# Half-block stores in the middle of a fused attention and MLP kernel, and two evacuations on other engines

## The chip, the cores and the metric

The kernel runs on one core of one Trainium2 chip. The metric is the device time of one execution in microseconds; the median of three runs before the change is 215.45 us (215.32 to 215.66).

## The reference

A lightning attention (linear attention with a decay per head, computed in blocks, with a running state) feeds an MLP with an ELU-like activation. Cut to what matters:

```python
# q, k, v: (4, 8, 768, 64); lam: one decay per head
for b in range(nb):                        # blocks along the sequence
    intra = einsum('bhic,bhjc->bhij', qb, kb) * Dmask       # causal, decayed
    intra = einsum('bhij,bhjd->bhid', intra, vb)
    inter = einsum('bhid,bhde->bhie', qb * lam_pow, kv_state)
    out[:, :, sl] = intra + inter
    kv_state = lam_block * kv_state + einsum('bhsd,bhse->bhde', kb * rev_pow, vb)
x = out as (3072 tokens, 512)
h = x @ w_in                               # 512 -> 2048
g = where(h > 0, h, exp(min(h, 0)) - 1)
y = g @ w_out                              # 2048 -> 512, float32, the output
```

## The kernel before, in words

**Tiling.** The 3072 tokens are 24 blocks of 128 (4 batches, 6 blocks of the sequence each, numbered g = 0 to 23). Everything stays on chip between attention and MLP. For a block the attention needs q and k transposed (T), the scores (S, line 302), the weighted values and the state's share (P, lines 338 and 344), and the state's update (U, line 406). The MLP's first matmul `mm1` (line 478) works on pairs of blocks, with an exponential and a ReLU on ScalarE (lines 484, 485) and a combination on VectorE (line 457); its second, `mm2` (line 499), gathers one block's 512 output columns in one PSUM bank in four steps.

**Order.** The order is written out by hand: a list of steps (`prog`) is run from front to back, and every engine executes its instructions in the order in which they were written. `1:g:j` is a step of `mm1`, `2:g:j` one of `mm2`, `S18:19` the scores of two blocks, `B:P18:...` their values and states. `W18` (`pool_work`) issues, for blocks from 8 on, the two transposes of block 18 (its q, then its k) as DMAs on SyncE (line 268); `L20` loads q, k and v of blocks 20 and 21 through GpSimd's queue (line 109). The part of the list around the change reads

```
... 2:12:3 1:14:3 W18 2:13:0 1:14:4 B:P16:P17:U16:U17 2:13:1 1:14:5 W19 2:13:2 1:14:6 L20 2:13:3
1:14:7 2:14:0 1:16:0 S18:19 2:14:1 1:16:1 2:14:2 1:16:2 2:14:3 1:16:3 W20 ...
```

**Stores.** When a block's fourth step of `mm2` is done, `out_of` copies its PSUM bank into an SBUF tile of 128 x 512 (`osb`, four buffers; line 525 on ScalarE) and appends a store to the list `stores`. Nothing is issued there. `mm1` calls `emit_stores(1)` at its beginning, which writes the DMA issues to SyncE (line 450) until one entry is left. A store thus stands in SyncE's order behind the evacuation of the next block, but waits only for its own evacuation. SyncE's order there, with T for two transposes, is: store 11, T18, T19, store 12, store 13, T20, T21, store 14, store 15, T22, T23, store 16 and on.

**The end.** The last block, 23, is computed in two parts: columns 0 to 383 by `mm2` (`CUT`), evacuated on VectorE (line 523), and columns 384 to 511 by `mm2_rest` (line 511), evacuated on ScalarE (line 525). For this block `out_of` issues its store at once.

**Completion.** The framework gives SyncE's DMAs eight landing semaphores in turn (in the trace: 108, 109, 113, 114, 115, 116, 117, 118). A later reader of the data, and a later writer of the tile, waits on the semaphore of the DMA in question. At the end of the program SyncE waits for all semaphores in a fixed order (line 658), among them these eight in the order given, before all engines meet and the program ends.

Of the kernel before, what the change touches and what calls it, by code (L numbers as in the profile page):

```python
# [7 lines left out]
FP32 = mybir.dt.float32  # L8
# [7 lines left out]
def kernel(  # L16
# [11 lines left out]
    nc = tc.nc  # L28

    B, H, S, D = q.shape  # L30
# [7 lines left out]
    FB = 4  # L38
    NJ = NFT // FB
    GPE = 8  # L40
    LAST = NG - 1
    CUT = 384
    GSIZE = {**{g: 1 for g in range(4)}, **{g: 2 for g in range(4, NG, 2)}}
    GFIRST = {g0 + i: g0 for g0, n in GSIZE.items() for i in range(n)}
    WI = [2] * 8
# [22 lines left out]
    TAGS = {w: t.replace(",", " ") for w, t in (x.split("=") for x in BANKS.split())}  # L68
# [7 lines left out]
    ps = ctx.enter_context(tc.tile_pool(name="ps", bufs=1, space=bass.MemoryType.PSUM))  # L76
# [36 lines left out]
    for w in RAW.split():  # L113
        x = {"q": q, "k": k}[w[0]]
        g0 = int(w[1:])
        raw[w] = asb.tile([128, H, 64], FP32, name=f"raw_{w}", tag=f"raw_{w}")
        (nc.sync if w[0] == "q" else nc.scalar).dma_start(
            out=raw[w][:], in_=x[g0, :, 0:L].rearrange("h p d -> p h d")
# [80 lines left out]
    def zero_st1(b):  # L199
# [21 lines left out]
        out=ident16[:], in0=row[:], scalar1=pos[:, 0:1], scalar2=None, op0=ALU.is_equal  # L221
    )
    nc.vector.tensor_scalar(
        out=causT[:], in0=row[:], scalar1=pos[:, 0:1], scalar2=None, op0=ALU.is_ge
# [24 lines left out]
    def bank(what, i, shape, dtype, name):  # L249
        tag = TAGS[what].split()[i]  # L250
        return ps.tile(
            shape, dtype, tag=f"ps{tag}", name=name, bufs=2 if tag == "H" else 1
        )
# [55 lines left out]
    def until(done, g):  # L309
        while g not in done:  # L310
            late.pop(0)()
# [15 lines left out]
    def att_P(g):  # L327
# [21 lines left out]
        def evacuate():  # L349
            g0 = GFIRST[g]  # L350
            n = GSIZE[g0]
            if g0 not in xg:
# [92 lines left out]
    gts, psM, stores, pending = {}, {}, [], []  # L445

    def emit_stores(keep=0):
        while len(stores) > keep:
            dst, o = stores.pop(0)
            nc.sync.dma_start(out=dst, in_=o)  # L450

    def flush():
        while pending:
            g0, j, e, r = pending.pop(0)
            n = GSIZE[g0]
            g = msb.tile([128, FB // n, n, 128], FP16, tag="g", bufs=40, name=f"g{g0}_{j}")
            nc.vector.scalar_tensor_tensor(  # L457
                out=g[:].rearrange("p f c t -> p (f c t)"), in0=e[:], scalar=-1.0, in1=r[:],
                op0=ALU.add, op1=ALU.min,
            )  # L460
            for f in range(FB // n):
                for c in range(n):
                    gts[(g0 + c, j * (FB // n) + f)] = g[:, f, c, :]
        if late:
            late.pop(0)()

    def mm1(g0, j):
        flush()
        emit_stores(1)
        n = GSIZE[g0]  # L470
        assert {f"P{g0 + i}" for i in range(n)} <= seen
        for i in range(n):
            until(X_done, g0 + i)
        pH = ps.tile([128, FB * 128], FP32, tag="psH", bufs=2, name=f"psH{g0}_{j}")
        for f in range(FB // n):
            i, w = wi_of[j * (FB // n) + f]
            for kk in range(NHP):
                nc.tensor.matmul(  # L478
                    pH[:, f * n * 128 : (f + 1) * n * 128],
                    lhsT=wi16[i][:, kk, w * 128 : (w + 1) * 128],  # L480
                    rhs=xg[g0][:, kk, :], start=(kk == 0), stop=(kk == NHP - 1),
                )
        e = msb.tile([128, FB * 128], FP32, tag="e", bufs=3, name=f"e{g0}_{j}")
        nc.scalar.activation(e[:], pH[:], AF.Exp)  # L484
        nc.scalar.activation(pH[:], pH[:], AF.Relu)  # L485
        pending.append((g0, j, e, pH))
# [3 lines left out]
    def mm2(g, j):  # L490
        flush()
        cols = slice(0, CUT if g == LAST else DM)
        if mm2_done[g] == 0:
            psM[g] = bank(f"M{g}", 0, [128, DM], FP32, f"psM{g}")
        first, mm2_done[g] = mm2_done[g] == 0, mm2_done[g] + 1
        end = mm2_done[g] == NJ
        for f in range(FB):
            i, w = wo_of[j * FB + f]
            nc.tensor.matmul(  # L499
                psM[g][:, cols], lhsT=gts[(g, j * FB + f)], rhs=wo16[i][:, w, cols],  # L500
                start=first and f == 0, stop=end and f == FB - 1, skip_group_check=True,
            )
        if end:
            out_of(g, psM[g][:, cols], cols, nc.vector if g == LAST else nc.scalar)

    def mm2_rest():
        cols = slice(CUT, DM)
        rest = ps.tile([128, DM - CUT], FP32, tag="psA", name="psMrest", bufs=1)
        for f in range(NFT):
            i, w = wo_of[f]  # L510
            nc.tensor.matmul(
                rest[:], lhsT=gts[(LAST, f)], rhs=wo16[i][:, w, cols],
                start=f == 0, stop=f == NFT - 1,
            )
        out_of(LAST, rest[:], cols, nc.scalar)

    def out_of(g, src, cols, eng):
        cb, b = divmod(g, B)
        t0 = b * S + cb * L
        w = cols.stop - cols.start  # L520
        o = msb.tile([128, w], FP32, tag=f"osb{w}", bufs=4, name=f"osb{g}_{cols.start}")
        if eng is nc.vector:
            eng.tensor_copy(o[:], src)
        else:
            eng.copy(o[:], src)  # L525
        stores.append((out[t0 : t0 + 128, cols], o[:]))
        if g == LAST:
            emit_stores()

# [26 lines left out]
    def run(t):  # L556
        w, *a = t[0], *t[1:].replace(":", " ").split()
        if w == "B":
            for o in a:
                ready(o)  # L560
            burst(*a)
            return
        a = [int(x) for x in a]
        if w in "PUzZ":
            ready(t)
        if w == "S":
            for g in a:
                att_S(g)
            for g in a:
                late.extend(att_E(g))  # L570
            late.pop(0)()
            late.pop(0)()
        elif w == "P":
            burst(t)
        elif w == "U":
            late.extend(att_U(*a))
            while late:
                late.pop(0)()
        else:
            {"T": att_T_pe, "1": mm1, "2": mm2, "Z": zero_st, "z": zero_st1,  # L580
             "q": lambda g, e: cast_raw(g, "q", e), "k": lambda g, e: cast_raw(g, "k", e),
             "c": lambda i: (emit_qs, emit_mask, emit_ks)[i](), "W": pool_work, "L": load_pair,
             "M": next_M, "w": zero_matmuls}[w](*a)

    for t in FIRST.split():
# [4 lines left out]
    done = set(prog) | {o for t in prog if t[0] == "B" for o in t.split(":")}  # L590
    m1 = [(g, j) for g, n in GSIZE.items() for j in range(NJ * n)]
    place = {u: i for i, u in enumerate(m1)}
    need = {
        (g, j): place[(GFIRST[g], ((j + 1) * FB - 1) // (FB // GSIZE[GFIRST[g]]))]
        for g in range(NG) for j in range(NJ)
# [31 lines left out]
    for t in prog:  # L627
        run(t)
    mm2_rest()
    while late:  # L630
        late.pop(0)()
# [31 lines left out]
```

## Time and profile before

| what | us |
|---|---|
| median of 3 runs | 215.45 |
| profiled execution, first to last instruction (span) | 213.2 |
| TensorE matmuls busy | 202.7 |
| VectorE busy | 130.1 |
| ScalarE busy | 129.0 |
| last matmul's end | 210.1 |
| last store issued | 210.41 |
| last store landed | 212.01 |
| last instruction's end | 213.2 |

The times in profile lines count from the first instruction of the span. Engines are named PE (TensorE matmuls), PEld (its weight loads), DVE (VectorE), ACT (ScalarE), POOL (GpSimd) and SP (SyncE); a q behind the name stands for the engine's sequencer, which issues DMAs and waits. `out<-in` are the names of tiles. In a timeline a row begins with its start and its length. A row with `x2` merges two neighbouring instructions of one kind, and its length then includes the time between them. In a list of waits the numbers are the total, the times and the longest. "DMA to landing" counts from the issue to the arrival of the whole transfer.

### The profile page before, as it was taken

How to read it: one execution, taken by the hardware profiler on the slowest of the kernel's cores; microseconds unless marked ns; L12 is line 12 of the kernel's file. 1: busy time of each engine (PE TensorE's matmuls, PEld its weight loads, DVE VectorE, ACT ScalarE, POOL GpSimd, SP SyncE). 2: the span in 40 equal slices, each digit the busy share in tenths (PEclk: the TensorE clock that was granted, in tenths of full speed). 3: DMA queues.
4: the chain of work that ended last, by engine and by line, in shares of the span. 5: the costliest groups of instructions: out<-in, count | busy, mean ns of one | idle time of the engine just before them, and what ended most of it. 6: DMA issues, size and time to landing. Idle time of an engine off the chain costs nothing.

```text
span 213.2 us, 5156 instructions
## 1 busy us (share of the span) xinstructions
PE 202.7 (95%) x2066; PEld 138.1 (65%) x2066; DVE 130.1 (61%) x224; ACT 129.0 (61%) x245; POOL 96.2 (45%) x115
## 2 busy tenths in 40 slices
PE   7667999999999999999999999999999999999994
PEld 2355676767686776766766766766766666666652
DVE  3936453777846888677667667667667547533321
ACT  4545654884867756676476476476476576477640
POOL 7996991999972908667166259300000000000000
PEclk9999999999999999999999999999999999999999
DMA  8999999999996999999939919999124110110112
GB/s 90 141 175 193 192 148 173 147 165 147 153 165 145 111 197 107 144 122 116 129 106 125 167 59 103 144 180 161 52 65 83 52 49 0 54 51 16 36 49 98
DMA packets 101976, 24.59 MB, mean 115 GB/s; under 512 B 92608, under 2 KB 99008, under 8 KB 101952
## 3 DMA queue, kind: packets, MB, share of 16 engines
q0 software_dynamic: 79760, 13.50, 83.1%
q1 hardware_dynamic: 22192, 10.76, 24.6%
q8 instruction: 16, 0.26, 0.5%
q14 instruction: 8, 0.07, 0.1%
HBM read 27.27 MB, written 6.29 MB: 157 GB/s over the span
## 4 chain that ended last, share of the span: by engine, by line
PE 82%; POOL 8%; DMA 7%; issue 1%; ACT 1%; DVE 0%; POOLq 0%; ACTq 0%
PE psM L499 36%; PE psH L478 35%; DMA wi<-in_moe_w_in_dram 4%; DMA wo<-in_moe_w_out_dram 3%; PE psO L338 3%; PE psS L302 3%; PE psO L344 2%; POOL kd L174 1%; POOL wi L148 1%; POOL kn L109 1%; POOL vn L109 1%; PE psU L406 1%; PE psT L283 1%; POOL qn L109 1%; POOL wo L155 1%
## 5 line engine op out<-in xcount | busy, mean ns | idle before, releaser
L478 PE MATMUL psH<-xt,wi 128*128 128x256 f16 (+1 forms) x896 | 99.3, 258 | 2.0 <-DMA wi<-in_moe_w_in_dram 1.1
L457 DVE SCALAR_TENSOR_TENSOR g<-e,psH 128x512 f16<-128x512 f32 x96 | 65.8, 686 | 56.7 <-ACT psH L485 56.0
L484 ACT ACTIVATE e<-psH 128x512 f32<-128x512 f32 x96 | 57.3, 597 | 65.0 <-PE psH L478 62.8
L499 PE MATMUL psM<-wo,g 128*128 128x512 f16 (+1 forms) x384 | 95.6, 377 | 0.7 <-DMA wo<-in_moe_w_out_dram 0.7
L478 PEld LDWEIGHTS <-wi 128*128 128x128 f16 x896 | 76.9, 98 | 27.4 <-DMA wi<-in_moe_w_in_dram 1.8
L485 ACT ACTIVATE psH<-psH 128x512 f32<-128x512 f32 x96 | 57.0, 593 | 0.0
L499 PEld LDWEIGHTS <-g 128*128 128x128 f16 x384 | 35.9, 98 | 29.3 <-issue 1.3
L318 DVE TENSOR_TENSOR pp<-psS,mask 128x512 f16<-128x512 f32 x48 | 30.8, 684 | 4.4 <-PE psS L302 4.4
L174 POOL TENSOR_TENSOR kd<-kn,ks 128x512 f16<-128x512 f16 x20 | 20.7, 1040 | 21.3 <-DMA kn<-in_k_dram 20.4
L378 POOL TENSOR_TENSOR stt<-st,upp 64x256 f32<-64x256 f16 x32 | 19.5, 608 | 14.7 <-DVE st L418 8.9
L109 POOL DMA_DIRECT2D vn<-in_v_dram x14 | 15.5, 1108 | 1.7 <-DMA wi<-in_moe_w_in_dram 1.7
L109 POOL DMA_DIRECT2D kn<-in_k_dram x14 | 15.5, 1105 | 0.8 <-POOLq L647 0.8
L525 ACT COPY osb<-psM 128x512 f32<-128x512 f32 x23 | 13.5, 590 | 3.2 <-PE psM L499 3.2
L109 POOL DMA_DIRECT2D qn<-in_q_dram x13 | 14.8, 1138 | 0.0
L418 DVE TENSOR_TENSOR st<-stt,psU 64x256 f16<-64x256 f32 x32 | 13.3, 416 | 1.2 <-PE psU L406 0.5
L361 DVE TENSOR_TENSOR xt<-psO,qs 128x512 f16<-128x512 f32 x16 | 11.0, 688 | 3.5 <-PE psO L344 3.5
L338 PE MATMUL psO<-pp,vn 128*64 128x128 f16 x192 | 12.0, 222 | 1.2 <-DMA vn<-in_v_dram 1.0
L338 PEld LDWEIGHTS <-vn 128*64 128x64 f16 x192 | 9.7, 110 | 4.6 <-issue 2.9
L344 PE MATMUL psO<-qT,st 128*64 128x128 f16 x160 | 10.0, 219 | 0.0
L344 PEld LDWEIGHTS <-st 128*64 128x64 f16 x160 | 8.9, 110 | 0.0
L302 PE MATMUL psS<-qT,kT 64*128 64x128 f16 x192 | 7.9, 218 | 0.3 <-ACT kT L291 0.3
L359 ACT CAST xt<-psO 128x512 f16<-128x512 f32 x8 | 4.4, 588 | 6.4 <-PE psO L338 4.3
(44 smaller groups left out, 72.3 us busy)
## 6 DMA issues: line engine op xcount, KB each, us to landing
out_dram<-osb SPq DMA_DIRECT2D x23, 256.0 KB, 2.2
kn<-in_k_dram POOLq DMA_DIRECT2D x10, 256.0 KB, 7.8
qn<-in_q_dram POOLq DMA_DIRECT2D x10, 256.0 KB, 6.8
vn<-in_v_dram POOLq DMA_DIRECT2D x10, 256.0 KB, 7.6
wi<-in_moe_w_in_dram POOLq DMA_DIRECT2D x8, 256.0 KB, 6.9
wo<-in_moe_w_out_dram POOLq DMA_DIRECT2D x8, 256.0 KB, 7.7
kn<-in_k_dram POOLq DMA_DIRECT2D x4, 128.0 KB, 4.2
vn<-in_v_dram POOLq DMA_DIRECT2D x4, 128.0 KB, 5.5
```

The source lines that it names most:

```text
L109: nc.gpsimd.dma_start(out=t[:].rearrange("p b h d -> p (b h) d"), in_=src)
L174: nc.gpsimd.tensor_tensor(out=kd[:], in0=of(kg, g), in1=ks[:].unsqueeze(2).broadcast_to([128, H, 64]), op=ALU.mult,)
L302: nc.tensor.matmul(psS[g][hh][:, hp, :], lhsT=kt[r, hp, :], rhs=qt[r, hp, :], start=True, stop=True,)
L318: nc.vector.tensor_tensor(out=P[:], in0=pts[hh][:], in1=mask[:, hh::2, :], op=ALU.mult)
L338: nc.tensor.matmul(po[r, hp, :], lhsT=vt[:, 2 * hp + hh, :], rhs=Pt[(g, hh)][:, hp, :], start=True, stop=(cb == 0), skip_group_check=True,)
L344: nc.tensor.matmul(po[r, hp, :], lhsT=st[b][cb % 2][:, hp, r], rhs=qt[:, hp, :], start=False, stop=True, skip_group_check=True,)
L378: nc.gpsimd.tensor_tensor(out=tmp[r], in0=old[r, :, r], in1=upp[r].unsqueeze(2).broadcast_to([64, NHP, 64]), op=ALU.mult,)
L457: nc.vector.scalar_tensor_tensor(out=g[:].rearrange("p f c t -> p (f c t)"), in0=e[:], scalar=-1.0, in1=r[:], op0=ALU.add, op1=ALU.min,)
L478: nc.tensor.matmul(pH[:, f * n * 128 : (f + 1) * n * 128], lhsT=wi16[i][:, kk, w * 128 : (w + 1) * 128], rhs=xg[g0][:, kk, :], start=(kk = ...
L484: nc.scalar.activation(e[:], pH[:], AF.Exp)
L485: nc.scalar.activation(pH[:], pH[:], AF.Relu)
L499: nc.tensor.matmul(psM[g][:, cols], lhsT=gts[(g, j * FB + f)], rhs=wo16[i][:, w, cols], start=first and f == 0, stop=end and f == FB - 1, ...
```

## The change

Blocks 12, 14, 15, 16 and 17 append two entries to `stores` in place of one, of 256 columns (128 KB) each; the evacuations are unchanged. The two parts of the last block swap engines: columns 0 to 383 are now copied by ScalarE, columns 384 to 511 by VectorE. A lookup of the PSUM tag for `mm1`'s tile is added; no entry of the table `BANKS` begins with H, so the tile stays where it was.

```diff
     CUT = 384
+    SPLIT = (12, 14, 15, 16, 17)
@@ mm1
-        pH = ps.tile([128, FB * 128], FP32, tag="psH", bufs=2, name=f"psH{g0}_{j}")
+        tag = TAGS.get(f"H{g0}_{j}", "H")
+        pH = ps.tile(
+            [128, FB * 128], FP32, tag=f"ps{tag}", name=f"psH{g0}_{j}",
+            bufs=2 if tag == "H" else 1,
+        )
@@ mm2
-            out_of(g, psM[g][:, cols], cols, nc.vector if g == LAST else nc.scalar)
+            out_of(g, psM[g][:, cols], cols, nc.scalar)
@@ mm2_rest
-        out_of(LAST, rest[:], cols, nc.scalar)
+        out_of(LAST, rest[:], cols, nc.vector)
@@ out_of
-        stores.append((out[t0 : t0 + 128, cols], o[:]))
+        parts = 2 if g in SPLIT else 1
+        for i in range(parts):
+            c = slice(i * w // parts, (i + 1) * w // parts)
+            d = slice(cols.start + c.start, cols.start + c.stop)
+            stores.append((out[t0 : t0 + 128, d], o[:, c]))
         if g == LAST:
             emit_stores()
```

## The prediction

> **What bounds the kernel now.** I read the page first, then the waits of TensorE's neighbours, then SyncE's queue, where the change acts, and last the end of the span.
>
> ```profile
> span 213.2 us, 5156 instructions
> PE 202.7 (95%) x2066; PEld 138.1 (65%) x2066; DVE 130.1 (61%) x224; ACT 129.0 (61%) x245; POOL 96.2 (45%) x115
> PE psM L499 36%; PE psH L478 35%; DMA wi<-in_moe_w_in_dram 4%; DMA wo<-in_moe_w_out_dram 3%; PE psO L338 3%; PE psS L302 3%; PE psO L344 2%; POOL kd L174 1%; POOL wi L148 1%; POOL kn L109 1%; POOL vn L109 1%; PE psU L406 1%; PE psT L283 1%; POOL qn L109 1%; POOL wo L155 1%
> ```
>
> TensorE is busy for 95% and carries the chain. In windows from 90 to 184 us it is busy without a gap, so whatever stops it there comes out at the end in full. ACT and VectorE have slack: in 120 to 204 us they wait 30.5 and 30.2 us for it.
>
> The changed stores are issued by SyncE, which works in program order and spends most of its time blocked (SyncE's waits):
>
> ```profile
> SPq L450 <- ACT osb L525: 131.1, 19, 40.9
> SPq L658 <- DMA out_dram<-osb: 1.1, 2, 0.8
> ```
>
> A store at the head of that queue waits for its evacuation, and everything behind it waits too. Behind some of them stand transposes that TensorE needs. SyncE's timeline (start, length, instruction):
>
> ```profile
> 126.03 0.33 SPq L450 DMA_DIRECT2D out_dram<-osb  x1
> 126.47 1.22 SPq L268 DMA_TRANSPOSE qT<-qn  x1
> 127.78 1.22 SPq L268 DMA_TRANSPOSE kT<-kn  x1
> 129.09 1.22 SPq L268 DMA_TRANSPOSE qT<-qn  x1
> 130.36 1.33 SPq L268 DMA_TRANSPOSE kT<-kn  x1
> 133.64 8.65 SPq L450 DMA_DIRECT2D out_dram<-osb  x2
> 142.39 1.25 SPq L268 DMA_TRANSPOSE qT<-qn  x1
> ```
>
> The store at 126.03 is block 11's; then T18 and T19 (two transposes each); the pair merged from 133.64 is the stores of blocks 12 and 13; T20 begins at 142.39. TensorE needs T18 and T19 here (its timeline), the second half of the 16 matmuls being block 19's, from 143.95:
>
> ```profile
> 143.64 0.62 PE L302 MATMUL psS<-qT,kT 64*128 64x128 f16 x16
> ```
>
> **The end of the span.** The last evacuation ends at 210.38, the 64 KB store issues at 210.41 and lands 1.60 later, at 212.01. SyncE's waits at L658 then go through the landing semaphores in a fixed order. Six start between 212.02 and 212.33, 0.061 apart: the first is the last store's own, the five behind it are for stores and engines long done.
>
> ```profile
> 209.23 0.56 DVE L523 COPY osb<-psM 128x384 f32<-128x384 f32 x1 [4.19 <-PE psM L499]
> 209.81 0.93 SPq L450 DMA_DIRECT2D out_dram<-osb  x2
> 210.12 0.27 ACT L525 COPY osb<-psMrest 128x128 f32<-128x128 f32 x1 [2.91 <-PE psMrest L511]
> ```
>
> **The change part by part.** *The ring.* SyncE issues 59 transfers (25 stores, 32 transposes, 2 loads) over eight landing semaphores in turn; the 59th takes the third. Five halves more make 64, and the 64th takes the eighth. The five waits then pass while the store is under way: 5 x 0.061 = **-0.30 us**.
>
> *The engines.* VectorE has no 128x128 copy out of PSUM in this trace. From its 128x384 copy (0.558) and its 64x256 cast (0.422) the slope is 1.06 ns an element, so 0.422 - 0.136 = 0.286 estimated, against ACT's 0.265: **+0.02** on the path. Bounds: its cast from SBUF (0.228) and its first 128x128 compare (0.377), so -0.04 to +0.11. The 384-column copy on ACT, interpolated between 0.265 and 0.590, is 0.48 against 0.56; its store moves up by 0.08, which is not on the path, but could free the last store's landing, so 0 to -0.08; I take 0. Both engines start 0.02 after TensorE's semaphore.
>
> *Five more issues.* 0.33 us each plus a wait of 0.05, 1.9 us of SyncE in all. SyncE's 68.1 us of waiting for evacuations from 120 us on hides them. ACT's evacuations of blocks 16 and 18 to 21 must wait for two landings instead of one (0.028 against 0.017): hidden in its 30.5 us of waiting. Without that cover all this is under 2.0 us.
>
> *The order on SyncE.* This is the term that decides. `emit_stores(1)` in `mm1` counts entries and leaves one behind. Today block 12's only entry stays behind until block 13 has been evacuated, and the W18 and W19 steps, which issue T18 and T19, are written in between. With two entries the list after block 12's evacuation is 11, 12a, 12b, and the next `mm1`, directly ahead of W18, issues 11 and 12a. So 12a, which must wait for its evacuation, moves **ahead of four transposes**; 14a does the same to T20 and T21, 16a to T22 and T23. 15 and 17 move past nothing.
>
> T18 now starts when 12a is out: 133.64 + 0.43 (the distance from block 11's store to T18) = 134.07 instead of 126.47. With the pitch of 1.30 the fourth is issued at 137.97. What does a transpose take to land? The first group is T19, at 129.09 and 130.36; the second T22 and T23, at 158 to 163:
>
> ```profile
> DMA to landing us min/median/max: 7.5/7.7/7.9
> ...
> DMA to landing us min/median/max: 2.4/2.4/2.5
> ```
>
> T19 runs beside GpSimd's loads, T22 beside nothing. And the loads are thick just there (GpSimd's timeline):
>
> ```profile
> 131.47 1.18 POOL L109 DMA_DIRECT2D qn<-in_q_dram  x1
> 132.60 1.19 POOL L109 DMA_DIRECT2D kn<-in_k_dram  x1
> 133.73 1.20 POOL L109 DMA_DIRECT2D vn<-in_v_dram  x1
> ```
>
> The last load lands at 145.16. At 2.45 the last transpose lands at 140.4 and nothing is lost; at 7.9, at 145.9. Better by the queue's pace: by the landing semaphores' records, pairs of transposes beside loads took 7.15 (98.37 to 105.52, from the landing ahead of them to their own), 6.43 (114.95 to 121.38) and 7.81 us (130.45 to 138.26), so 3.2 to 3.9 each, 3.6 in the middle. The loads of 128 to 145 are 12,384 packets; alone they run at 1,230 per us (141 to 143 us), beside transposes at 644 (131.6 to 136.9). Undisturbed until 134.6 they have done some 4,900 (350 by 130.9, then 1,230 per us); the other 7,500 at 644 to 705 (the mean of 130 to 138.2) end at 145.2 to 146.2. 12a takes about 1 us (half of store 12's 2.4, from 138.26 to 140.65), so by then some 2.8 transposes have landed and the rest follows alone, at 0.5 (T20's first two landings) to 1.3 each: 146.5 in the middle, 145 to 148. TensorE waits from 143.95: **+2.55 us**, nothing else being late, since the same engine carries the rest and every later step shifts with it.
>
> [...]
>
> For T20 and T22 no loss: from 149.99 and 165.92 the fourth lands 6.35 later, at 156.3 and 172.3, and is needed at 159.57 and 175.24. The DMA share has fallen from 2.45 to 0.27 by 148 us; beside loads these would be late too.
>
> Sum: -0.30 + 0.02 + 2.55 = +2.27 us. On the profiled execution 213.2 becomes 215.5; the median lies 2.2 above the span, so 215.45 + 2.27 = **217.7 us**.
>
> **Rivals.** (1) *The transposes land in time.* Place: T19's second landing against 143.95. Price: no stall, only the end's -0.28, **215.2**. It decides if a transpose takes under 2.1 us beside loads (8.35 us for four from 135.6). For it: 2.45 alone and 3.5 us of margin; T19's two landings were only 1.6 apart. Against: no pair in the trace went under 6.4. (2) *The stall also drops the clock.* After the last matmul at 210.1 the granted clock fell at 212.8, 2.7 later; at the start ten matmuls took 4.00 us (0.40 each, later ones 0.22) until the clock came up after 3.4. A gap a little over 2.7 would cost half of 3.4 more, 1.7: **219.4**. Against: eight of the sixteen matmuls can run within the gap. [...] (3) *The ring doesn't fall as counted*, and the end keeps its waits: **218.0**.
>
> **How the numbers follow.** Forecast (stall of 0.7 us and more, clock kept) 0.67; rival 1 with stalls under 0.7 0.20; rival 2 0.09; rival 3 0.04. About 0.2%, 0.43 us, is what a measurement of this kernel can tell from no change. Rival 1 lies mostly inside it, since its -0.28 is 0.13%: same 0.15, faster 0.05; all else is slower, 0.80. The forecast alone runs from 216.4 to 219.2 (landing 145.2 to 148); with rival 1 and rival 2's centre taken in, 215.1 to 219.4.
>
> **What would show it.** Right: SyncE's store near 133.64 followed at once by four transposes, their landings up to 146 or later, a gap of TensorE before L302 near 143.9 put down to a DMA of kT or qT, all later pieces shifted by it; one wait of L658 after the last landing in place of six. Wrong: no such gap, with landings before 144; or transposes still at 126.

## The result, and the profile after

| | median, us | lowest to highest | runs |
|---|---|---|---|
| before | 215.38 | 214.61 to 215.66 | 6 |
| changed | 217.34 | 216.96 to 219.51 | 6 |

The changed kernel is slower: ratio 1.0113, 95% interval 1.0076 to 1.015, with 217.7 us forecast. The profiled execution took 218.70 us, its span 216.9; the rest around the span is 1.8 us. Ratios are of fast executions; only e3 below had slow ones, two of eight at 219.38 and 219.88 us, which its ratio leaves out.

The page of the changed kernel (its `mm1` stands on line 483 now, the scores on 303, SyncE's stores on 451 and its transposes on 269):

```profile
span 216.9 us, 5161 instructions
PE 206.4 (95%) x2066; PEld 140.7 (65%) x2066; DVE 129.9 (60%) x224; ACT 129.3 (60%) x245; POOL 96.3 (44%) x115
PEclk9978999999999999999999999996999999999999
PE psH L483 39%; PE psM L504 37%; DMA kT<-kn 3%; PE psS L303 3%; PE psO L339 3%; DMA qn<-in_q_dram 3%; PE psO L345 2%; PE psT L284 1%; POOL kn L110 1%; PE psU L407 1%; ACT e L489 1%; POOL vn L110 1%; ACT psH L490 1%; DVE g L458 1%; PE psMrest L516 0%
L303 PE MATMUL psS<-qT,kT 64*128 64x128 f16 x192 | 8.3, 221 | 2.6 <-DMA kT<-kn 2.2
```

Two things are new. `DMA kT<-kn` now carries 3% of the chain that ended last, and it ends 2.2 us of TensorE's idle time before the scores. And the row of the granted clock has a 6 in its 28th slice, in the middle of a kernel that ran at full clock there before (the 7 and the 8 near the row's start are another drop, from 14.01 to 17.42 us, long before the change acts). The row of the kernel before:

```profile
PEclk9999999999999999999999999999999999999999
```

SyncE's timeline shows where the waiting comes from:

```profile
125.77 7.94 SPq L451 DMA_DIRECT2D out_dram<-osb  x2
133.81 1.29 SPq L269 DMA_TRANSPOSE qT<-qn  x1
135.19 2.01 SPq L269 DMA_TRANSPOSE kT<-kn  x1
137.30 1.30 SPq L269 DMA_TRANSPOSE qT<-qn  x1
138.65 1.70 SPq L269 DMA_TRANSPOSE kT<-kn  x1
```

The merged row from 125.77 is store 11 and, at 133.38, store 12a; T18 and T19 follow it. Their four landings are at 142.01, 144.12, 144.89 and 146.04. TensorE's timeline at the same place:

```profile
144.16 0.40 PE L303 MATMUL psS<-qT,kT 64*128 64x128 f16 x8 [0.72 <-DMA kT<-kn]
146.09 0.40 PE L303 MATMUL psS<-qT,kT 64*128 64x128 f16 x8 [1.53 <-DMA kT<-kn]
146.42 1.24 PE L504 MATMUL psM<-wo,g 128*128 128x512 f16 x4
147.45 1.91 PE L483 MATMUL psH<-xt,wi 128*128 128x256 f16 x8
```

The sixteen score matmuls have come apart into two groups, each behind a transpose of k: block 18's waits for the landing at 144.12, block 19's for that at 146.04. Two rows below, eight matmuls of `mm1` take 1.91 us; they took 1.04 before. A window of 3.3 us there (busy time by engine, then clock, DMA share, GB/s):

```profile
147.20:150.50 3.30, 3.30 (x14) 1.68 (x12) 0.61 (x2) 1.04 (x2) 0.00 (x0) 0.50 0.00 0
```

The clock stands at 0.50, from 147.13 to 150.54 by its own records.

The span grew by 3.70 us, and it divides so. Up to the scores this execution is 0.26 ahead. The scores end at 146.49 instead of 144.26, so the gap cost 2.23 + 0.26 = 2.49. TensorE's last semaphore comes 3.90 later than before, so the half clock cost 3.90 - 2.23 = 1.67. From there to the end it is 2.93 against 3.13, so the end gave back 0.20. The last rows:

```profile
213.13 0.48 ACT L530 COPY osb<-psM 128x384 f32<-128x384 f32 x1 [2.01 <-PE psM L504]
213.63 1.04 SPq L451 DMA_DIRECT2D out_dram<-osb  x2
214.02 0.29 DVE L528 COPY osb<-psMrest 128x128 f32<-128x128 f32 x1 [5.08 <-PE psMrest L516]
```

The last store lands at 216.01, SyncE's wait for it starts at 216.02, and the next instruction is the final drain at 216.09: the five waits are gone from behind it.

### The profile page after: what moved, and what is told of

Same layout as the page of the kernel before. It is cut to its first block, busy times and chain, and to the rows that moved or that the text cites. A ratio compares the mean times of both kernels' runs of the same rounds, so it can differ in the third digit from the quotient of the medians.

```text
span 216.9 us, 5161 instructions
## 1 busy us (share of the span) xinstructions
PE 206.4 (95%) x2066; PEld 140.7 (65%) x2066; DVE 129.9 (60%) x224; ACT 129.3 (60%) x245; POOL 96.3 (44%) x115
## 4 chain that ended last, share of the span: by engine, by line
PE 86%; DMA 6%; POOL 3%; ACT 2%; DVE 1%; issue 1%; SPq 0%; POOLq 0%; ACTq 0%
PE psH L483 39%; PE psM L504 37%; DMA kT<-kn 3%; PE psS L303 3%; PE psO L339 3%; DMA qn<-in_q_dram 3%; PE psO L345 2%; PE psT L284 1%; POOL kn L110 1%; PE psU L407 1%; ACT e L489 1%; POOL vn L110 1%; ACT psH L490 1%; DVE g L458 1%; PE psMrest L516 0%
## 5 line engine op out<-in xcount | busy, mean ns | idle before, releaser
L483 PE MATMUL psH<-xt,wi 128*128 128x256 f16 (+1 forms) x896 | 100.9, 261 | 1.4 <-ACT xt L360 1.0
L483 PEld LDWEIGHTS <-wi 128*128 128x128 f16 x896 | 78.7, 100 | 26.9 <-issue 2.6
L530 ACT COPY osb<-psM 128x512 f32<-128x512 f32 (+1 forms) x24 | 14.0, 585 | 5.2 <-PE psM L504 5.2
L303 PEld LDWEIGHTS <-kT 64*128 64x128 f16 x192 | 5.7, 95 | 5.6 <-DMA kT<-kn 2.7
```

What stands on the lines that cost most here:

```text
L303: nc.tensor.matmul(psS[g][hh][:, hp, :], lhsT=kt[r, hp, :], rhs=qt[r, hp, :], start=True, stop=True,)
L483: nc.tensor.matmul(pH[:, f * n * 128 : (f + 1) * n * 128], lhsT=wi16[i][:, kk, w * 128 : (w + 1) * 128], rhs=xg[g0][:, kk, :], start=(kk = ...
```

## The experiments

Each ran beside the kernel before on the same chip. Ratios have 95% intervals. "End" is the stretch from TensorE's last semaphore to the end of the span in the profiled execution.

| run | SyncE's order | ratio | wait before the scores, us | end, us |
|---|---|---|---|---|
| before | T18, T19, 12 | 1 | none | 3.13 |
| changed | 12a, T18, T19 | 1.0113 [1.0076, 1.015] | 0.72 + 1.53 | 2.93 |
| e1 halves together | T18, T19, 12a, 12b | 0.9994 [0.9973, 1.0015] | none | 2.91 |
| e2 whole 12 early | 12, T18, T19 | 1.0117 [1.0072, 1.0163] | 0.22 + 1.98 | 3.13 |
| e3 only 12 in halves | 12a, T18, T19 | 1.0102 [1.0065, 1.0139] | 0.56 + 1.52 | 3.06 |
| e4 14, 16 in halves | 14a, T20; 16a, T22 | 0.9994 [0.9968, 1.002] | none | 2.91 |
| e5 no loads for 22, 23 | 12a, T18, T19 | 0.9991 [0.9973, 1.0009] | none | 2.90 |
| e6 18 to 22 in halves | as before | 1.0003 [0.998, 1.0025] | none | 2.91 |
| e7 as e6, old engines | as before | 0.9992 [0.9968, 1.0016] | none | 2.89 |
| e8 swap alone | as before | 0.9998 [0.9974, 1.0022] | none | 3.13 |
| e9 changed, again | 12a, T18, T19 | 1.0112 [1.0072, 1.0151] | 2.26 | 2.93 |
| e10 changed, filler matmuls | 12a, T18, T19 | 1.0088 [1.0054, 1.0122] | filled | 2.91 |
| e11 T18, T19 behind 13 | 12, 13, T18, T19 | 1.031 [1.0271, 1.0348] | 2.48 + 2.22 | 3.11 |

**e1: the same halves, the old order.**

```diff
+        entry = []
         for i in range(parts):
...
-            stores.append((out[t0 : t0 + 128, d], o[:, c]))
+            entry.append((out[t0 : t0 + 128, d], o[:, c]))
+        stores.append(entry)
@@ emit_stores
-            dst, o = stores.pop(0)
-            nc.sync.dma_start(out=dst, in_=o)
+            for dst, o in stores.pop(0):
+                nc.sync.dma_start(out=dst, in_=o)
```

> The five blocks are still stored in halves and the engines stay swapped, but both halves of a block are issued together, so that SyncE's order is that of the kernel before (store 11, T18, T19, 12a, 12b, 13, ...). 64 transfers as in the changed kernel. Theory (the order on SyncE makes the loss): transposes at 126 us again, landings by 138.3, no gap of TensorE before the scores near 143.9, one wait after the last landing instead of six: 0.2 us under the kernel before, ratio 0.9985 to 1.000. Rival (halves as such cost: more transfers, smaller rows): still 1.5 to 2.5 us over the kernel before, ratio 1.007 to 1.012.

SyncE's and TensorE's timelines of this run:

```profile
126.60 0.33 SPq L451 DMA_DIRECT2D out_dram<-osb  x1
127.04 1.22 SPq L269 DMA_TRANSPOSE qT<-qn  x1
...
144.21 0.62 PE L303 MATMUL psS<-qT,kT 64*128 64x128 f16 x16
```

With the same 64 transfers and the same halves, but the transposes straight behind store 11 again, the scores are one group of sixteen and the loss is gone. Halves as such cost nothing that these times show.

**e2: the old kernel, whole store 12 early.**

```diff
-        emit_stores(1)
+        emit_stores(0 if (g0, j) == (14, 3) else 1)
```

> The kernel before, with one edit: block 12's whole store is issued ahead of T18 and T19. No halves, no swap, 59 transfers. Theory: the transposes start at 134 us and the last lands at 146 to 147.5, since a whole store of 256 KB stands ahead of them; TensorE waits 2.2 to 3.5 us, and the clock may drop behind it, 1.7 more: ratio 1.009 to 1.020. Rival (halves as such cost): no change, ratio 0.998 to 1.002.

SyncE's timeline (the merged row is stores 11 and 12) and TensorE's:

```profile
125.73 7.94 SPq L450 DMA_DIRECT2D out_dram<-osb  x2
133.77 1.28 SPq L268 DMA_TRANSPOSE qT<-qn  x1
...
143.63 0.40 PE L302 MATMUL psS<-qT,kT 64*128 64x128 f16 x8 [0.22 <-DMA kT<-kn]
146.00 0.40 PE L302 MATMUL psS<-qT,kT 64*128 64x128 f16 x8 [1.98 <-DMA kT<-kn]
```

One moved issue in the old kernel, with no half, no swap and no other ring position, makes the whole loss (1.0117 against 1.0113). With e1 this settles the cause from both sides.

**e3 and e4: which of the moved halves costs.**

```diff
-    SPLIT = (12, 14, 15, 16, 17)
+    SPLIT = (12,)                      # e3
+    SPLIT = (14, 16, 18, 19, 20)       # e4
```

> The changed kernel with block 12 alone in halves: 12a stands ahead of T18 and T19, 14 and 16 go back behind their transposes. 60 transfers, so the last store takes the fourth semaphore and four waits stand behind it. Theory: the whole loss is there: gap of 2.2 to 2.5 us near 143.9, ratio 1.008 to 1.016. Rival (14a and 16a cost as well): under half of the loss, ratio 1.002 to 1.005.

> The changed kernel with blocks 14, 16, 18, 19 and 20 in halves: 14a and 16a stay ahead of T20, T21 and T22, T23, block 12 is whole again; 64 transfers. Theory: T18 and T19 are back at 126 us, the four transposes behind 14a and 16a meet no loads and land at 156.3 and 172.3, about 3 us before their scores at 159.6 and 175.2: no gap, 0.2 us under the kernel before, ratio 0.9985 to 1.000. Rival (every half ahead of transposes costs): 1 to 2 us over, ratio 1.005 to 1.010.

Block 12 alone makes it. In e4 the moved transposes stand behind 14a and 16a. SyncE's rows at 14a, and TensorE's scores of blocks 20 and 21:

```profile
150.16 0.33 SPq L451 DMA_DIRECT2D out_dram<-osb  x1
150.63 1.19 SPq L269 DMA_TRANSPOSE qT<-qn  x1
151.93 1.20 SPq L269 DMA_TRANSPOSE kT<-kn  x1
153.65 1.23 SPq L269 DMA_TRANSPOSE qT<-qn  x1
154.94 2.21 SPq L269 DMA_TRANSPOSE kT<-kn  x1
...
160.16 0.62 PE L303 MATMUL psS<-qT,kT 64*128 64x128 f16 x16
```

T21 lands at 158.41, 1.75 us ahead of its scores, T23 at 173.64, 2.2 ahead of 175.84. Nothing is lost, but the margin is smaller than the 3 us expected, in part because one issue took 2.21 us and one 1.99 where I had counted 1.3.

**e5: the same order without half of the loads.** Blocks 22 and 23 reuse the q, k and v tiles of blocks 20 and 21.

```diff
     def load_pair(g):
+        if g == 22:
+            for t in (qg, kg, vg):
+                t[22] = t[20]
+            return
```

> The changed kernel without the loads of q, k and v for blocks 22 and 23: these blocks reuse the tiles of blocks 20 and 21, so half of GpSimd's packets of 128 to 145 us are gone, and SyncE's order stays as changed (12a ahead of T18 and T19). Theory (late issue hurts only beside the loads): the remaining 6,200 packets are done by about 136, the four transposes are still issued from 134 to 138 but land by 141 to 142, before 143.6: no gap, ratio 0.997 to 1.000. Rival (the late issue is enough by itself): the gap stays at 2 us and more, ratio 1.008 to 1.012.

From the view of SyncE's transposes, T18 and T19, in the changed kernel and then in this run:

```profile
DMA to landing us min/median/max: 7.4/7.9/8.9
```

```profile
DMA to landing us min/median/max: 2.5/2.9/4.0
```

They were issued from 133.56, as late as in the changed kernel, and the last landed at 139.92, over 3 us ahead of the scores, which are one group again:

```profile
143.12 0.62 PE L303 MATMUL psS<-qT,kT 64*128 64x128 f16 x16
```

So late issue cost time here only together with GpSimd's loads. This time also lacks three loads, so it is no comparison for the whole kernel.

**e6, e7 and e8: what the end is worth.**

```diff
-    SPLIT = (12, 14, 15, 16, 17)
+    SPLIT = (18, 19, 20, 21, 22)       # e6 and e7
@@ mm2                                  # e7, of e6
-            out_of(g, psM[g][:, cols], cols, nc.scalar)
+            out_of(g, psM[g][:, cols], cols, nc.vector if g == LAST else nc.scalar)
@@ mm2_rest                             # e7, of e6
-        out_of(LAST, rest[:], cols, nc.vector)
+        out_of(LAST, rest[:], cols, nc.scalar)
```

e8 is the kernel before with only the two lines of `mm2` and `mm2_rest` changed as in the change.

> The changed kernel with blocks 18 to 22 in halves in place of 12 and 14 to 17: no transpose is left behind these stores, 64 transfers, engines swapped. Theory: SyncE's order up to store 17 is the old one, no gap; one wait after the last landing; the stretch from TensorE's last semaphore to the end of the span is 2.93 us as in the changed kernel, 3.13 before: 0.2 us under, ratio 0.998 to 1.000. Rival (halves close to the end hold up the last stores): the last landing is later by 0.2 us and more, ratio 1.000 to 1.002.

> As the run with blocks 18 to 22 in halves, but the last block's 384 columns stay on VectorE and its 128 on ScalarE, as before. Theory: the waits' 0.30 us are saved without the swap's cost (0.03 for the copy, 0.06 for the landing): from TensorE's last semaphore to the end 2.83 us, ratio 0.997 to 1.000. Rival (the swap is what brings the end forward): 3.0 us and more.

> The kernel before with the two last evacuations swapped and nothing else, 59 transfers. Theory: 128 columns on VectorE take 0.29 us against 0.265, the last store lands 0 to 0.06 later: from TensorE's last semaphore to the end 3.16 to 3.22 us against 3.13, ratio 0.999 to 1.002. Rival (the earlier store of 384 columns lets the last one land earlier): 3.05 us and less.

The ring moves the end from 3.13 to 2.91 (e6) or 2.89 (e7), and the swap alone moves nothing (e8, 3.13, where I had expected 3.16 to 3.22): the copy on VectorE took 0.292 against 0.265, the landing 1.586 against 1.596. I had expected 2.83 in e7. What is missing is in the landing: 1.67 from issue to landing here, 1.60 before. The gain of 0.2 us, 0.1%, is less than the runs of any pair can tell apart; no version is shown to beat the kernel before by its time.

**e9, e10 and e11: the clock.** In e10 TensorE gets work to do in the gap; in e11, made from the kernel before, the gap is made long.

```diff
     for t in prog:
+        if t == "S18:19":
+            zero_matmuls(8)            # e10
         run(t)
```

```diff
-        if g >= GPE:                   # e11, in pool_work
+        if g >= GPE and g not in (18, 19):
             att_T_dma(g)
@@ mm1
-        emit_stores(1)
+        emit_stores(0 if (g0, j) == (16, 0) else 1)
+        if (g0, j) == (16, 0):
+            att_T_dma(18)
+            att_T_dma(19)
```

> The changed kernel as it is, beside the next two on the same chip. Theory (the gap of 2 to 2.5 us lies near what the clock stands, so that it drops in some executions and costs 1.7 us there): times in two groups, some 216.8 to 217.7 and some 218.5 to 219.5, the upper ones with a lower mean clock. Rival (the upper times come from the start of the kernel): they appear as often without a gap.

> The changed kernel with eight matmuls on zeros (1.73 us, results unused) put on TensorE ahead of the scores of blocks 18 and 19, so that it is busy while it would wait. Theory (clock drop in some executions): no gap over 1 us is left and the clock stays, so the times keep to one group, 216.5 to 217.7, since the scores still start when the last transpose has landed near 146; median a little under the changed kernel's. Rival (the upper times come from elsewhere): as many times over 218.4 as in the changed kernel. If the fillers end after the landing, at most 0.5 us more.

> The kernel before with T18 and T19 issued behind stores 12 and 13 in place of ahead of store 12; nothing else moves, 59 transfers. They start at 142.4, where T20 stood, and should land as T20 and T21 did, up to 149.9. Theory: TensorE waits from 143.95 for 5.9 us less 0.3 for the first half of the scores, and the clock drops behind it in every execution, 1.7 us more: 222 to 223, ratio 1.031 to 1.039. Rival (a gap alone doesn't drop the clock): 220.5 to 221.2, ratio 1.025 to 1.029.

The changed kernel gave 216.67 to 218.92 (median 217.51), with one of six above 218.4, where two of six had been in the first measurement; the two groups of times that I had expected do not show. In e10 the filler took the gap's place, and the scores are one group:

```profile
143.05 1.89 PE L85 MATMUL psZ<-zero 128*128 128x512 f16 x8 [0.22 <-DVE g L458]
144.87 0.62 PE L303 MATMUL psS<-qT,kT 64*128 64x128 f16 x16
```

All nine times with it were between 216.00 and 218.18 (median 216.66), and their mean granted clock was 0.998 to 1.000, while five of six without it were at 0.991 or 0.992. That agrees with the theory, but the times do not prove it. The two ranges overlap; the kernel before, which has no such gap, ran from 214.04 to 216.42 beside them, and four of its fourteen executions were at 0.989 to 0.992 as well, so a low mean does not say where the clock fell. The profiles say it: behind the gap in the changed kernel (0.50 from 147.13 to 150.54 us) and in e9 (0.50 in the window from 146.4 to 149.7). e2 (1.00 from 147.2 to 150.5) and e3 (a mean of 1.000) kept the clock with nearly the same gaps, 0.22 + 1.98 and 0.56 + 1.52. How much of the upper times is the clock, and how much comes from the start of the kernel (the rival), stays open.

The long gap of e11 gave 221.6, between the two expectations: its transposes landed by 148.95, 0.9 ahead of the 149.9 expected, and its clock did fall (two windows of e11, before and after the end of the gap):

```profile
145.40:148.70 3.30, 0.40 (x8) 0.23 (x8) 1.88 (x3) 0.00 (x0) 0.00 (x0) 1.00 0.50 102
148.80:152.10 3.30, 3.10 (x17) 1.57 (x18) 1.29 (x2) 0.00 (x0) 0.00 (x0) 0.50 0.60 84
```

## Why the prediction held, step by step

- **The order on SyncE** was read rightly from `emit_stores(1)`: 12a went ahead of T18 and T19. T18 was put at 134.07 and came at 133.81, in an execution that ran 0.26 ahead. e1, e2 and e3 show that this one move is the loss.
- **The stall** was put at 2.55 and came to 2.49, the last landing at 146.5 and 146.04. The parts behind it were off and cancelled, which was luck. I let 12a through in about 1 us from 134.6; in fact only the loads' queue moved from 134 to 137, and 12a landed at 139.96. The four transposes then came 2.05, 2.11, 0.77 and 1.15 apart, where I had put 3.6 for each that shared the queues with loads. What held was the end of the loads, put at 145.2 to 146.2; the last one landed at 145.86.
- **Loads as the condition**: shown by e5, where the same late transposes took 2.9 us in the middle instead of 7.9.
- **T20 and T22 free of loss**: right (e4), though with 1.75 and 2.2 us of margin instead of 3.
- **The clock** was held to stay in the forecast, with 0.09 for a drop; no trace had shown what a gap of 2.55 does to it. That was too low: it fell in both profiles of the changed kernel and cost 1.67 us in the first. Rival 2 is a part of the result, not its alternative: with nearly the same gap the profiles of e2 and e3 kept the clock. What this adds to the spread of the times (216.67 to 219.51) is not shown, since the kernel before spreads by 2.4 us without a gap. Rival 2's bound of 2.7 failed here: gaps of 2.25 (0.72 + 1.53) and, in e9, 2.26 were enough.
- **The end**: the waits gave their 0.30, the swap cost 0.03 (0.286 estimated for VectorE's copy, 0.291 measured; 0.48 estimated for ScalarE's, 0.480 measured), and the last landing came 0.07 later, which I had not counted. 0.20 is left.
- **The way from span to time** was taken as 2.2 us, from a median and another execution's span; an execution's own time stands 1.8 above its span.
- **The number**, 217.7 against 217.34, says less than it seems to. In the profiled execution the forecast's own terms came to 2.29 (2.49 less 0.20) and the clock added 1.67. The median rose by 1.96, where 2.27 was forecast; which of the other executions lost clock behind the gap no trace shows.
- **A reading that was off**: VectorE's 30.2 us of waiting were for ScalarE (line 485), not for TensorE. Nothing in the sum hangs on it.

## What to carry to other kernels

SyncE issued in program order here, and a store that was blocked was a gate for all behind it: T18 came at 133.81 in place of 126.47 us. Before a store is split, count which entries of its list now pass which loads or transposes, and look up when those are needed. What a transfer costs at a later time hung on what the DMA queues carried there: the same late transposes took 7.9 us in the middle beside the loads and 2.9 without half of them (e5). Take a duration from a row at that place, not from a quiet median (2.4 for T22 and T23 in the kernel before). And a gap of two microseconds on TensorE was priced twice in the profile of the changed kernel, 2.49 us as waiting and 1.67 in the clock behind it; in that of e2, with 0.22 + 1.98, it was priced once.

## What the runs showed of the hardware that was not expected

**When the clock falls.** In the traces of both kernels the clock's records go by steps of 3.413 us: the stretches of full clock of 208.21 us (the kernel before), 129.71 and 68.27 us (the changed one) are 61, 38 and 20 of them, and each drop within the changed kernel's span, at 14.01 and at 147.13, lasted one. The steps did not start with the program: TensorE's first matmul starts at 1.19 us in both, the first record of full clock at 4.61 in the kernel before and at 7.18 in the changed one. So I counted TensorE's idle time step by step. In the changed kernel the step from 143.71 to 147.13 held 1.98 us of it and was followed by half clock; so was the step from 10.59 to 14.01, with 2.22, and at the end of the kernel before the one from 209.41 to 212.82, with 2.74. Of the steps that kept the clock, the one with the most idle time is that of the kernel before from 4.61 to 8.02, with 1.70. By these two traces the limit is put between 1.70 and 1.98 idle of 3.41, an estimate, as far as the profile's modelled ends of matmuls go. e9 and e11 agree: half clock from 146.4 to 149.7 in e9 stands behind a gap that lasted from 144.15 to 146.41, and in e11 TensorE was busy for 0.40 of the 3.30 us from 145.40, ahead of the 0.50 from 148.80. That e2 and e3 kept the clock would then be a matter of how their gaps lay to the steps, which is an estimate as well.

**Who gets the DMA queues.** Where SyncE's queue was filled anew while the loads were under way, the loads' packets alone were moved for 1.9 and 4.1 us. The changed kernel from 134 to 137 us, with 12a and T18 issued from 133.38 on (packets by queue):

```profile
DMA packets 3463, 0.44 MB, mean 147 GB/s; under 512 B 3463, under 2 KB 3463, under 8 KB 3463
q0 software_dynamic: 3463, 0.44, 229.7%
```

SyncE's queue, q1, has no line there; its first packet behind the issue starts at 137.48. Nor has it one in the kernel before from 142 to 143.8 us (2,216 packets of the loads), where store 13 was issued at 141.96; there the first starts at 143.85. Earlier in the same kernel, where T19 was still under way on q1, it moved 556 packets beside 1861 of the loads from 134 to 137 us. Why, and whether 12a's packets stood ready all that time, no trace shows.

**The last landing.** In the profiles of the changed kernel (e9 too), e1, e4, e6, e7 and e10, where the last store had the eighth semaphore, it took 1.66 to 1.67 us from issue to landing (1.64 in e5); with the third or fourth, in the kernel before, e2, e3, e8 and e11, 1.58 to 1.60. Why was not tried.
